# Loading taps and first expert weights in halves of 64 partitions between pairs of x loads

## The chip, the cores and the metric

The kernel runs on one core of a Trainium2 chip. The metric is the time of one execution on the device in microseconds; the time before is the median of three runs. The profile is of one execution, and its times count from the start of its span.

## The reference

A per-head softmax over seven taps weights a causal window of seven tokens; the result goes through a soft mixture of eight experts with four slots each.

```
# x: (8, 3584, 192), weight_gen: (8, 3584, 8 heads, 7 taps)
w = exp(weight_gen - max over taps);  w = w / (sum over taps + 1e-9)
out[b,s,h,:] = sum over k of w[b,s,h,k] * x_padded[b, s+k, h,:]     # six zeros ahead of x
x2 = out.reshape(28672, 192)
logits = x2 @ phi                                   # 32 slots
d = exp(logits - max over tokens); d = d / (sum over tokens + 1e-9)
slot_input = d.T @ x2                               # (8 experts, 4 slots, 192)
slot_out[e] = relu(slot_input[e] @ w1[e]) @ w2[e]   # F = 1024
c = softmax over slots of logits
return c @ slot_out
```

## The kernel before

The work has three stages. The first runs the convolution, the logits and a running softmax over tokens (an online maximum with rescaling, so that `d.T @ x2` is summed as the tokens pass). The second runs the experts on 32 slots. The third multiplies the per-token slot weights with the experts' outputs and stores the result.

**Tiling of the first stage.** A batch's 3584 tokens are cut into tiles of 26; each needs 32 rows of x. Sixteen tiles make an x tile in SBUF, loaded in four DMAs of 32 partitions each (`loadx`, L156): DMA h fills partitions 32h to 32h+31 with the heads h of both halves of the model dimension, so that x stands as a block diagonal whose other blocks were zeroed once. There are 69 x tiles in a ring of five slots (`NXS`). Four tiles make a group, two groups a pair; TensorE works in 35 blocks of four pairs, so a block uses two x tiles. The weights of the convolution come in 35 chunks, one for each block. A chunk's taps are one load over 128 partitions (`loadw`, L160) into one of three buffers. Then follow a chain over three engines: VectorE's maximum (`top`, L171), GpSimd's subtraction (L175), ScalarE's exponential (L179), GpSimd's sum in three steps (L188 to L190), VectorE's reciprocal (L194), GpSimd's product into `wide` (L202), and VectorE's transposition into one of three `band` buffers (L206). TensorE's convolution of a block (`cv`, L230) reads the chunk's band and two x tiles. In each second block TensorE also computes the logits of a unit of eight pairs (`ls`, L281); VectorE takes their maximum (`mx`, L288; `mq`, L290), TensorE spreads it over the partitions (`acb`, L306), VectorE reduces it (`nm`, L310), ScalarE takes exponentials and TensorE sums the slots' inputs (`acb`, L346). The transpositions `pt` (L250) stand between.

**What sets the order.** All loads are issued by SyncE (SP), one after the other, in the order in which the program lists them. For block k the list has: the taps of chunk k+4 (for k = 0, of chunks 3 and 4), the x tiles 2k+5 and 2k+6 (for k = 0 tiles 4 and 5, then `phi`, then tile 6), and now and then a piece of the first expert weights (w1a for the first 128 rows of w1, w1b for the other 64), of which 24 pieces of 128 partitions are spread over the x tiles, two for five tiles. An x tile waits until its slot's old tile was convolved, a chunk's taps until the buffer's old chunk was exponentiated. TensorE's order is the list's too. The orders on VectorE, ScalarE and GpSimd are made by a planner in the kernel (`model`): it goes through the listed operations with a cost and a delay for each, takes at each step the most urgent one that is ready by its own account, and the engines then run that order as it stands. A change to loads in the list therefore changes the order on these engines too.

`op` states for each operation what it reads and writes by names, such as `("w", buffer, half of the chunk)` for taps and `x_of(t)` for an x tile.

Of the kernel before, what the change touches and what calls it, by code (L numbers as in the profile page):

```python
# [30 lines left out]
NS, E, SE, F = 32, 8, 4, 1024  # L31
# [14 lines left out]
def place(t):  # L46
    return t % NXS if t else NXS - 1
# [3 lines left out]
def conv_soft_moe(ctx, tc, xh, wh, phi, w1a, w1b, w2, out):  # L51
    nc = tc.nc
    V, A, G, P, SY = nc.vector, nc.scalar, nc.gpsimd, nc.tensor, nc.sync
# [57 lines left out]
    NTM, NCV, NPT, NTAP, NEX, NBAND = 2, 3, 3, 3, 2, 3  # L111
# [3 lines left out]
    taps = [fix.tile([128, CH, T, KT], F32, name=f"taps{i}") for i in range(NTAP)]  # L115
# [34 lines left out]
    qneg = keep.tile([128, 4], F32, name="qneg")  # L150
    q0 = keep.tile([128, 1], F32, name="q0")
    mq = keep.tile([128, 5], F32, name="mq")
    def loadx(t):

        for h in range(4):
            SY.dma_start(xbd[32 * h : 32 * h + 32, place(t), h], xh[t, h])  # L156

    def loadw(c):
        n = min(CH, NG // 4 - CH * c)
        SY.dma_start(taps[c % NTAP][:, 0:n], wh[c, :, 0:n])  # L160

    ALL = slice(0, CH)
    tops, tsums = {}, {}

    def each(t, n):
        return t.unsqueeze(3).to_broadcast([128, n, T, KT])

    def tap_top(c, b=ALL):
        n = b.stop - b.start
        m = tops[c, b.start] = pa.tile([128, CH, T], F32, tag="top", name=f"top{c}_{b.start}")[:, 0:n]  # L170
        V.tensor_reduce(out=m, in_=taps[c % NTAP][:, b], axis=AX.X, op=ALU.max)  # L171

    def tap_sub(c, b=ALL, eng=G):
        t = taps[c % NTAP][:, b]
        eng.tensor_tensor(out=t, in0=t, in1=each(tops.pop((c, b.start)), b.stop - b.start),  # L175
                          op=ALU.subtract)

    def tap_exp(c, b=ALL):
        A.activation(exps[c % NEX][:, b, :, 0:KT], taps[c % NTAP][:, b], AF.Exp)  # L179
# [11 lines left out]

    def tap_inv(c, b=ALL):
        m = tsums[c, b.start]
        V.reciprocal(m, m)  # L194

    def tap_mul(c, b=ALL, eng=G):

        n = b.stop - b.start
        m = tsums[c, b.start][:, 0:n] if (c, b.start) in tsums else tsums[c, 0][:, b]
        w = wide[:, b]  # L200
        dst = bass.AP(w.tensor, w.offset, [w.ap[0], [T * 32, n], [33, T], [1, KT]])
        eng.tensor_tensor(out=dst, in0=exps[c % NEX][:, b, :, 0:KT], in1=each(m, n), op=ALU.mult)  # L202
# [212 lines left out]
        SY.dma_start(w2_at(e, 0, FC), w2[:, e])  # L415

    def pace(e, what, src):
        op(PO, 0.15, [what], [("w2", e), x_of(NSG - NXS + e // 2)], mark, e, src)
        op(SP, 0.4, [("w2", e)], [], loadw2, e)

    logit, dispatched = {}, {}
    for u in range(1, final + 1):
        k, n = UNITS[u][0] // Q, -(-UNITS[u][1] // Q)
# [27 lines left out]

    VE, AC, PO, TE, SP = "VE", "AC", "PO", "TE", "SP"
    op(SP, 0.65, [], [("w", 0, 0), ("w", 0, 1)], loadw, 0, late=2.6)
    op(SP, 0.65, [], [("w", 1, 0), ("w", 1, 1)], loadw, 1, late=2.6)
    op(SP, 2.6, [], [x_of(0)], loadx, 0, late=2.8)
    op(SP, 0.6, [], [("w", 2, 0), ("w", 2, 1)], loadw, 2, late=3.0)
    op(SP, 1.9, [], [x_of(1)], loadx, 1, late=3.0)
    for t, es in ((2, (PO, AC, AC, AC)), (3, (PO, AC, VE, AC)), (NXS, (PO, PO, AC, AC))):
        for h, e in enumerate(es):
            op(e, 0.77, [], [("z", t, h)], clear, place(t), h, {PO: G, AC: A, VE: V}[e])  # L460
        if t < NXS:
            op(SP, 1.9, [("z", t, h) for h in range(4)], [x_of(t)], loadx, t, late=3.0)
# [82 lines left out]
    for k in range(BLOCKS):  # L545
        ps = range(Q * k, min(Q * (k + 1), PAIRS))
        for p in ps:
            if p == ps[0] + 3 and k in dispatched:
                weigh(dispatched[k])
            if p == ps[min(2, len(ps) - 1)] and k in logit:  # L550
                scores(logit[k])
            op(TE, 0.75 if p == ps[0] else 0.72, conv_reads(p), [("cv", p % NCV)], conv, p)
            op(AC, 0.48, [], [("cv", p % NCV), tm_of(p)], conv_out, p)
        for c in range(3, NCH):
            if k == max(0, c - 2):
                chain(c)
        for c in range(NTAP, NCH):
            if k == max(0, c - 4):
                op(SP, 0.4, [], [("w", c % NTAP, b) for b in range(CH)], loadw, c, late=4.0)
        for t in range(NSG):  # L560
            if (SGG * t + SGG - 1) // (2 * Q) == k:
                if t + NXS < NSG:
                    for i in (NXS - 1, NXS) if t == 0 else (t + NXS,):
                        op(SP, 2.0, [("z", i, h) for h in range(4)], [x_of(i)], loadx, i, late=3.0)
                    if t == 0:
                        op(SP, 0.45, [], ["phi"], SY.dma_start, phi_sb, phi, late=3.0)
                for j in range(2 * (E + E // 2)):
                    if 2 + 5 * j // 2 == t:
# [21 lines left out]
    v, n = final - 1, UNITS[final][1]  # L590
# [86 lines left out]
    for e, cost, late, preds, *_ in ops:  # L677
        t = max([free.get(e, 4.0)] + [goal[j] + ops[j][1] + ops[j][2] + HOP for j in preds])
# [43 lines left out]
    h = EARLY  # L722
# [109 lines left out]
    late = sorted((4 * i + k, h, k) for i, h in enumerate(range(EARLY + 3, len(STEPS))) for k in range(7))  # L832
# [99 lines left out]
```

## Time and profile before

| | us |
|---|---|
| median of three runs | 310.02 |
| lowest and highest run | 309.0, 312.22 |
| the profiled execution's own time | 308.94 |
| its span in the profile | 307.2 |
| first stage, until the last convolution | 222 |
| experts | from about 222 to 250 |
| output | from about 250 to the end |

The profiled execution takes 1.74 us more than its span. Of the data, 46.21 MB are read and 22.04 MB written. A waiting time in the profile's list of waits is idle time of the engine just ahead of the instruction that is named first, and what is named second ended it.

### The profile page before, as it was taken

How to read it: one execution, taken by the hardware profiler on the slowest of the kernel's cores; microseconds unless marked ns; L12 is line 12 of the kernel's file. 1: busy time of each engine (PE TensorE's matmuls, PEld its weight loads, DVE VectorE, ACT ScalarE, POOL GpSimd, SP SyncE). 2: the span in 40 equal slices, each digit the busy share in tenths (PEclk: the TensorE clock that was granted, in tenths of full speed). 3: DMA queues.
4: the chain of work that ended last, by engine and by line, in shares of the span. 5: the costliest groups of instructions: out<-in, count | busy, mean ns of one | idle time of the engine just before them, and what ended most of it. 6: DMA issues, size and time to landing. Idle time of an engine off the chain costs nothing.

```text
span 307.2 us, 15262 instructions
## 1 busy us (share of the span) xinstructions
PE 265.4 (86%) x6646; PEld 213.6 (70%) x6646; DVE 197.8 (64%) x337; ACT 190.3 (62%) x399; POOL 146.5 (48%) x254
## 2 busy tenths in 40 slices
PE   8898996999998999899899989999999888899100
PEld 8887975889887988789788878898768622233000
DVE  8867738775975957868478568573158489994100
ACT  9886673767685778667566666675422188786300
POOL 8856456654568194774654553520027345540000
PEclk9999998999999999999999999999999999879555
DMA  6758666867675767767567667657647079999994
GB/s 184 217 171 236 201 199 195 208 178 207 197 211 150 225 188 207 207 192 212 168 183 212 189 185 211 189 156 227 217 121 296 2 303 403 399 398 398 399 399 177
DMA packets 30161, 69.24 MB, mean 225 GB/s; under 512 B 6288, under 2 KB 11152, under 8 KB 30096
## 3 DMA queue, kind: packets, MB, share of 16 engines
q1 hardware_dynamic: 30096, 68.28, 69.2%
q8 instruction: 52, 0.85, 1.1%
q14 instruction: 13, 0.11, 0.1%
HBM read 46.21 MB, written 22.04 MB: 222 GB/s over the span
## 4 chain that ended last, share of the span: by engine, by line
PE 73%; DVE 6%; DMA 6%; issue 5%; ACT 2%; POOL 2%; DVEq 0%; POOLq 0%; ACTq 0%
PE cv L230 31%; PE pt L250 15%; PE ls L281 8%; PE acb L346 8%; PE po L818 5%; DMA out<-big 4%; PE so L763 2%; PE hpb L742 2%; PE acb L306 2%; DMA taps<-wh 2%; DVE big L825 1%; ACT big L825 1%; DVE band L206 1%; DVE big L362 1%; DVE cT L404 1%
## 5 line engine op out<-in xcount | busy, mean ns | idle before, releaser
L230 PE MATMUL cv<-big,band 128*26 128x96 f32 x4416 | 112.0, 250 | 4.0 <-issue 2.6
L230 PEld LDWEIGHTS cv<-big,band 128*26 128x26 f32 x4416 | 100.8, 130 | 13.8 <-issue 8.1
L236 ACT COPY tm<-cv 128x384 f32<-128x384 f32 x138 | 66.5, 484 | 62.8 <-PE cv L230 62.5
L206 DVE STREAM_TRANSPOSE band<-wide 128x1664 f32<-128x1664 f32 (+1 forms) x37 | 65.4, 1771 | 6.1 <-POOL wide L202 6.0
L250 PE MATMUL pt<-ident,tm 122*128 122x122 f32 x414 | 51.0, 273 | 0.0
L257 ACT COPY cm<-pt 128x416 f32<-128x416 f32 x103 | 48.1, 512 | 1.7 <-PE pt L250 0.6
L250 PEld LDWEIGHTS pt<-ident,tm 122*128 122x128 f32 x414 | 44.7, 145 | 2.3
L202 POOL TENSOR_TENSOR wide<-exps,sum 128x364 f32<-128x364 f32 (+1 forms) x36 | 28.4, 791 | 24.9 <-DVE sum L194 18.6
L818 PE MATMUL po<-cT,so 32*128 32x442 f32 (+3 forms) x256 | 35.4, 644 | 5.6 <-DVE big L825 3.0
L175 POOL TENSOR_TENSOR taps<-taps,top 128x364 f32<-128x364 f32 (+1 forms) x36 | 28.5, 793 | 18.3 <-DVE top L171 17.9
L825 ACT COPY big<-po 128x884 f32<-128x884 f32 (+2 forms) x33 | 28.5, 894 | 9.3 <-PE po L818 5.3
L188 POOL TENSOR_TENSOR si<-exps 128x208 f32<-128x208 f32 x32 | 20.2, 632 | 28.4 <-ACT exps L179 28.0
L818 PEld LDWEIGHTS po<-cT,so 32*128 32x128 f32 (+1 forms) x256 | 12.3, 172 | 27.5 <-ACT big L825 15.7
L281 PE MATMUL ls<-cm,phi_sb 128*32 128x208 f32 x544 | 29.1, 338 | 2.0 <-issue 1.9
L346 PE MATMUL acb<-tm,dt 128*32 128x193 f32 x544 | 27.4, 328 | 3.3 <-issue 3.3
L288 DVE TENSOR_REDUCE mx<-ls 128x1 f32<-128x416 f32 x17 | 10.0, 588 | 28.1 <-PE ls L281 28.1
L87 POOL TENSOR_TENSOR LT<-LT,rm 128x544 f32<-128x544 f32 (+1 forms) x16 | 17.9, 1119 | 17.0 <-DVE rm L85 17.0
L171 DVE TENSOR_REDUCE top<-taps 128x52 f32<-128x364 f32 (+1 forms) x37 | 17.7, 484 | 12.8 <-DMA taps<-wh 12.0
L281 PEld LDWEIGHTS ls<-cm,phi_sb 128*32 128x32 f32 x544 | 17.8, 109 | 7.9 <-issue 3.6
L346 PEld LDWEIGHTS acb<-tm,dt 128*32 128x32 f32 x544 | 17.8, 110 | 7.4 <-issue 4.7
L99 POOL TENSOR_TENSOR LT<-LT,sm 128x544 f32<-128x544 f32 (+1 forms) x16 | 17.9, 1120 | 6.3 <-DVE sm L97 6.2
L825 DVE COPY big<-po 128x884 f32<-128x884 f32 (+2 forms) x16 | 16.7, 1047 | 6.2 <-ACT big L825 2.2
(113 smaller groups left out, 262.3 us busy)
## 6 DMA issues: line engine op xcount, KB each, us to landing
big<-xh SPq DMA_DIRECT2D x276, 96.0 KB, 3.2
out<-big SPq DMA_DIRECT2D x36, 442.0 KB, 6.9
taps<-wh SPq DMA_DIRECT2D x34, 182.0 KB, 3.7
big<-w SPq DMA_DIRECT2D x8, 768.0 KB, 4.5
out<-big SPq DMA_DIRECT2D x11, 468.0 KB, 4.7
w1a_sb<-w1a SPq DMA_DIRECT2D x16, 256.0 KB, 4.2
w1b_sb<-w1b SPq DMA_DIRECT2D x8, 256.0 KB, 3.6
out<-big SPq DMA_DIRECT2D x2, 234.0 KB, 2.3
```

The costliest lines, as they stand in the source:

```text
L175: eng.tensor_tensor(out=t, in0=t, in1=each(tops.pop((c, b.start)), b.stop - b.start), op=ALU.subtract)
L188: eng.tensor_tensor(out=s, in0=t[:, :, :, 0:4], in1=t[:, :, :, 4:8], op=ALU.add)
L202: eng.tensor_tensor(out=dst, in0=exps[c % NEX][:, b, :, 0:KT], in1=each(m, n), op=ALU.mult)
L206: V.transpose(bands[c % NBAND][:, b].rearrange("p b j l -> p (b j l)"), wide[:, b].rearrange("p b j -> p (b j)"))
L230: P.matmul(cv[32 * blk : 32 * blk + T, o : o + 4 * GW], bands[g // 8 % NBAND][:, g // 4 % CH, :, i], xbd[:, place(t), :, b * GW : (b + 1) ...
L236: copy(tms[u % NTM][:, pr, 1 : 2 * D + 1], cvs[p % NCV][:, 0 : 2 * D])
L250: P.transpose(pt[:, at, 0:TR], tms[u % NTM][0:TR, pr, 1 + 128 * i : 129 + 128 * i], ident[0:TR, 0:TR])
L257: copy(cms[u].rearrange("p a i b j -> p (a i b) j")[:, at : at + n], pts.pop((k, j)).rearrange("p i (b j) -> p (i b) j", j=32)[:, 0:n, 0:T])
L281: P.matmul(lp[32 * blk : 32 * blk + 32, lo:hi, par, 0:T], phi_sb[:, 2 * par + i, :], cm[:, lo:hi, 1 if i else 2 * par, blk, :], start=(i = ...
L346: P.matmul(ac[32 * q : 32 * q + 32], dt[:, g, :], tm[:, g // 2, o : o + D + 1], start=(g < 4), stop=(g + 4 >= 2 * n))
L818: P.matmul(po[dst : dst + hi - lo, at, 0 : n * T], so[32 * q : 32 * q + 32, lo:hi], cT[32 * q : 32 * q + 32, g0 : g0 + n, 0:T], start=True ...
L825: (V.tensor_copy if done[1] % 3 == 1 else A.copy)(ot.rearrange("p (q c) -> p q c", c=n * T), po[:, 0 : len(qs), 0 : n * T])
```

## The change

`loadx` takes a range of DMAs to issue, `loadw` a range of partitions. For k above 0 each x tile is now issued as two pairs of DMAs (partitions 0 to 63, then 64 to 127), and one half of a chunk's taps stands between the pairs: partitions 0 to 63 in the first x tile of a block, 64 to 127 in the second. What is left of the list goes behind the x tiles: for k = 0 this is the second half of chunk 3 and both halves of chunk 4. The first expert weights come in 48 pieces of 64 partitions in place of 24 of 128, four for five x tiles. The first three chunks are loaded as before. An x tile has two names, one for each pair of DMAs; the convolution reads both.

```diff
-    def loadw(c):
+    def loadw(c, r=slice(0, 128)):
         n = min(CH, NG // 4 - CH * c)
-        SY.dma_start(taps[c % NTAP][:, 0:n], wh[c, :, 0:n])
+        SY.dma_start(taps[c % NTAP][r, 0:n], wh[c, r, 0:n])
+
+    def loadw1(j):
+        e, f, r = j // 4, slice(F // 2 * (j // 2 % 2), F // 2 * (j // 2 % 2 + 1)), HALF[j % 2]
+        to, w, e = (w1a_sb, w1a, e) if e < E else (w1b_sb, w1b, e - E)
+        SY.dma_start(to[r, e, f], w[r, e, f])
+    HALF = slice(0, 64), slice(64, 128)
...
-        for c in range(NTAP, NCH):
-            if k == max(0, c - 4):
-                op(SP, 0.4, [], [("w", c % NTAP, b) for b in range(CH)], loadw, c, late=4.0)
-        for t in range(NSG):
-            if (SGG * t + SGG - 1) // (2 * Q) == k:
-                if t + NXS < NSG:
-                    for i in (NXS - 1, NXS) if t == 0 else (t + NXS,):
-                        op(SP, 2.0, [("z", i, h) for h in range(4)], [x_of(i)], loadx, i, late=3.0)
-                    if t == 0:
-                        op(SP, 0.45, [], ["phi"], SY.dma_start, phi_sb, phi, late=3.0)
-                for j in range(2 * (E + E // 2)):
-                    if 2 + 5 * j // 2 == t:
...
+        cs = [c for c in range(NTAP, NCH) if k == max(0, c - 4)]
+        parts = [(c, i) for c in cs for i in range(2)]
+        for t in (2 * k, 2 * k + 1):
+            for i in (NXS - 1, NXS) if t == 0 else (t + NXS,) if t + NXS < NSG else ():
+                for j in range(2):
+                    op(SP, 1.0, [("z", i, h) for h in (2 * j, 2 * j + 1)], [x_of(i)[j]],
+                       loadx, i, (2 * j, 2 * j + 1), late=3.0)
+                    if j == 0 and parts and t:
+                        c, h = parts.pop(0)
+                        op(SP, 0.4, [], [("w", c % NTAP, h)], loadw, c, HALF[h], late=4.0)
+            if t == 0:
+                op(SP, 0.45, [], ["phi"], SY.dma_start, phi_sb, phi, late=3.0)
+            if 2 <= t < NSG:
+                for j in range(48):
+                    if 2 + 5 * j // 4 == t:
+                        op(SP, 0.42, [], [], loadw1, j)
+        for c, h in parts:
+            op(SP, 0.4, [], [("w", c % NTAP, h)], loadw, c, HALF[h], late=4.0)
```

**SP at the start.** The three tap buffers are taps_84 (chunks 0, 3, 6 and so on), taps_85 (chunks 1, 4) and taps_86 (chunks 2, 5). Before, behind the taps of chunk 2:

```order
L156 DMA big<-xh 32x768 x12
L160 DMA taps_84<-wh 128x364
L160 DMA taps_85<-wh 128x364
L156 DMA big<-xh 32x768 x8
L686 DMA phi_sb<-phi 128x128
L156 DMA big<-xh 32x768 x4
L160 DMA taps_86<-wh 128x364
```

Now, behind the taps of chunk 2 (the rows up to chunk 5's second half):

```order
L156 DMA big<-xh 32x768 x20
L695 DMA phi_sb<-phi 128x128
L156 DMA big<-xh 32x768 x2
L160 DMA taps_84<-wh 64x364
L156 DMA big<-xh 32x768 x2
L160 DMA taps_84<-wh 64x364
L160 DMA taps_85<-wh 64x364 x2
L156 DMA big<-xh 32x768 x2
L160 DMA taps_86<-wh 64x364
L156 DMA big<-xh 32x768 x2
L165 DMA w1a_sb<-w1a 64x512
L156 DMA big<-xh 32x768 x2
```

Chunks 3 and 4 stood ahead of x tiles 4, 5, `phi` and x tile 6 and now stand in and behind tile 6; the next row after these is chunk 5's second half, which stood behind tile 6 as a whole and now stands in tile 8.

**VectorE at the start.** The rows from the reciprocal of chunk 2 to the band of chunk 3 (band_90), before:

```order
L194 RECIPROCAL sum_0_325<-sum_0_325 128x52
L171 TENSOR_REDUCE top_0_387<-taps_84 128x52
L171 TENSOR_REDUCE top_0_390<-taps_85 128x52
L206 STREAM_TRANSPOSE band_92<-wide 128x1664
L194 RECIPROCAL sum_0_453<-sum_0_453 128x52
L288 TENSOR_REDUCE mx_525<-ls 128x1
L290 TENSOR_SCALAR mq<-ls,mx_525 128x4
L206 STREAM_TRANSPOSE band_90<-wide 128x1664
```

Now:

```order
L212 STREAM_TRANSPOSE band_92<-wide 128x1664
L294 TENSOR_REDUCE mx_510<-ls 128x1
L296 TENSOR_SCALAR mq<-ls,mx_510 128x4
L177 TENSOR_REDUCE top_0_534<-taps_84 128x52
L316 TENSOR_REDUCE nm_544<-acb 128x1
L177 TENSOR_REDUCE top_0_553<-taps_85 128x52
L333 STREAM_TRANSPOSE dt_564<-dd 128x512
L300 STREAM_TRANSPOSE LT<-ls 128x512
L200 RECIPROCAL sum_0_570<-sum_0_570 128x52
L177 TENSOR_REDUCE top_0_589<-taps_86 128x52
L200 RECIPROCAL sum_0_580<-sum_0_580 128x52
L212 STREAM_TRANSPOSE band_90<-wide 128x1664
```

The maxima of chunks 3 and 4 moved behind the first unit's `mx`, and the band of chunk 3 now stands behind the maximum of chunk 5 (taps_86).

**VectorE at the third unit's maximum.** The rows around the maxima of chunks 8 (taps_86) and 9 (taps_84) and the band of chunk 7 (band_91), before:

```order
L171 TENSOR_REDUCE top_0_928<-taps_86 128x52
L85 TENSOR_REDUCE rm_947<-LT 128x18
L354 SCALAR_TENSOR_TENSOR accS<-accS,al_949,acb 128x193
L194 RECIPROCAL sum_0_951<-sum_0_951 128x52
L171 TENSOR_REDUCE top_0_998<-taps_84 128x52
L206 STREAM_TRANSPOSE band_91<-wide 128x1664
L288 TENSOR_REDUCE mx_1064<-ls 128x1
L290 TENSOR_SCALAR mq<-ls,mx_1064 128x4
```

Now:

```order
L177 TENSOR_REDUCE top_0_963<-taps_86 128x52
L360 SCALAR_TENSOR_TENSOR accS<-accS,al_956,acb 128x193
L200 RECIPROCAL sum_0_958<-sum_0_958 128x52
L212 STREAM_TRANSPOSE band_91<-wide 128x1664
L294 TENSOR_REDUCE mx_1072<-ls 128x1
L296 TENSOR_SCALAR mq<-ls,mx_1072 128x4
L93 TENSOR_REDUCE sm_1093<-LT 128x18
L316 TENSOR_REDUCE nm_1105<-acb 128x1
L200 RECIPROCAL sum_0_1050<-sum_0_1050 128x52
L177 TENSOR_REDUCE top_0_1120<-taps_84 128x52
```

The maximum of chunk 9 moved from ahead of `mx` to behind it.

More of the change, by code (lines that the diff above doesn't have):

```diff
@@ L152, in conv_soft_moe, with loadx @@
     mq = keep.tile([128, 5], F32, name="mq")
-    def loadx(t):
-        for h in range(4):
+    def loadx(t, hs=range(4)):
+        for h in hs:
             SY.dma_start(xbd[32 * h : 32 * h + 32, place(t), h], xh[t, h])
-    def loadw(c):
+    def loadw(c, r=slice(0, 128)):
         n = min(CH, NG // 4 - CH * c)
-        SY.dma_start(taps[c % NTAP][:, 0:n], wh[c, :, 0:n])
+        SY.dma_start(taps[c % NTAP][r, 0:n], wh[c, r, 0:n])
[3 more added lines that the diff above has]
+        SY.dma_start(to[r, e, f], w[r, e, f])
     ALL = slice(0, CH)
+    HALF = slice(0, 64), slice(64, 128)
     tops, tsums = {}, {}
@@ L417, in pace @@
     def pace(e, what, src):
-        op(PO, 0.15, [what], [("w2", e), x_of(NSG - NXS + e // 2)], mark, e, src)
+        op(PO, 0.15, [what], [("w2", e), *x_of(NSG - NXS + e // 2)], mark, e, src)
         op(SP, 0.4, [("w2", e)], [], loadw2, e)
@@ L442, in x_of @@
     def x_of(t):
-        return ("x", place(t))
+        return [("x", place(t), i) for i in range(2)]
     def conv_reads(p):
-        return {x_of(g // SGG) for g in (2 * p, 2 * p + 1)} | {("band", p // 4 % NBAND, p // 2 % CH)}
+        return {x for g in (2 * p, 2 * p + 1) for x in x_of(g // SGG)} | {("band", p // 4 % NBAND, p // 2 % CH)}
     def tm_of(p):
@@ L454, in conv_soft_moe @@
     op(SP, 0.65, [], [("w", 1, 0), ("w", 1, 1)], loadw, 1, late=2.6)
-    op(SP, 2.6, [], [x_of(0)], loadx, 0, late=2.8)
+    op(SP, 2.6, [], x_of(0), loadx, 0, late=2.8)
     op(SP, 0.6, [], [("w", 2, 0), ("w", 2, 1)], loadw, 2, late=3.0)
-    op(SP, 1.9, [], [x_of(1)], loadx, 1, late=3.0)
+    op(SP, 1.9, [], x_of(1), loadx, 1, late=3.0)
     for t, es in ((2, (PO, AC, AC, AC)), (3, (PO, AC, VE, AC)), (NXS, (PO, PO, AC, AC))):
@@ L461, in conv_soft_moe @@
         if t < NXS:
-            op(SP, 1.9, [("z", t, h) for h in range(4)], [x_of(t)], loadx, t, late=3.0)
+            op(SP, 1.9, [("z", t, h) for h in range(4)], x_of(t), loadx, t, late=3.0)
     for i in range(NCV):
@@ L556, in conv_soft_moe @@
                 chain(c)
-        for c in range(NTAP, NCH):
-            if k == max(0, c - 4):
-                op(SP, 0.4, [], [("w", c % NTAP, b) for b in range(CH)], loadw, c, late=4.0)
-        for t in range(NSG):
-            if (SGG * t + SGG - 1) // (2 * Q) == k:
-                if t + NXS < NSG:
-                    for i in (NXS - 1, NXS) if t == 0 else (t + NXS,):
-                        op(SP, 2.0, [("z", i, h) for h in range(4)], [x_of(i)], loadx, i, late=3.0)
-                    if t == 0:
-                        op(SP, 0.45, [], ["phi"], SY.dma_start, phi_sb, phi, late=3.0)
-                for j in range(2 * (E + E // 2)):
-                    if 2 + 5 * j // 2 == t:
-                        e, f = j // 2, slice(F // 2 * (j % 2), F // 2 * (j % 2 + 1))
-                        to, w, e = (w1a_sb, w1a, e) if e < E else (w1b_sb, w1b, e - E)
-                        op(SP, 0.4, [], [], SY.dma_start, to[:, e, f], w[:, e, f])
+        cs = [c for c in range(NTAP, NCH) if k == max(0, c - 4)]
[16 more added lines that the diff above has]
+            op(SP, 0.4, [], [("w", c % NTAP, h)], loadw, c, HALF[h], late=4.0)
         for p in ps:
```

## The prediction

> **What bounds the kernel now.** I read the page first, then the busy time of each engine by stretches, then the chain of waits, and last the timelines of SP, VectorE and TensorE around the places where the chain leaves TensorE. The page's busy shares and its chain, by engine:
>
> ```profile
> PE 265.4 (86%) x6646; PEld 213.6 (70%) x6646; DVE 197.8 (64%) x337; ACT 190.3 (62%) x399; POOL 146.5 (48%) x254
> PE 73%; DVE 6%; DMA 6%; issue 5%; ACT 2%; POOL 2%; DVEq 0%; POOLq 0%; ACTq 0%
> ```
>
> The stretches of the first stage and of the output (length, busy time of PE, PEld, DVE, ACT, POOL, granted clock, DMA share, GB/s):
>
> ```profile
> 13.00:50.00 37.00, 32.47 (x992) 28.46 (x992) 24.57 (x36) 26.09 (x61) 20.81 (x38) 1.00 0.68 198
> 50.00:100.00 50.00, 48.05 (x1347) 42.41 (x1351) 36.12 (x60) 32.72 (x75) 32.26 (x54) 0.97 0.68 195
> 100.00:150.00 50.00, 47.60 (x1417) 41.87 (x1412) 35.70 (x60) 34.34 (x79) 28.28 (x49) 1.00 0.70 203
> 150.00:205.00 55.00, 53.35 (x1585) 47.56 (x1577) 38.70 (x61) 37.09 (x83) 26.30 (x49) 1.00 0.65 187
> 250.00:307.20 57.20, 30.77 (x228) 10.68 (x224) 30.13 (x44) 29.76 (x42) 14.17 (x13) 0.73 0.95 369
> ```
>
> TensorE bounds the first stage: it is idle 4.5 us between 13 and 50, and 1.95 + 2.4 + 1.65 = 6.0 us between 50 and 205. The last row is the output, where the DMAs are busy 95% of the time; the change leaves the experts and the output alone. So a gain can come only from some 10.5 us of idle TensorE in the first stage, and a loss from new idle time there.
>
> **Term 1, the start.** SP's timeline, before:
>
> ```profile
> 9.58 1.25 SPq L160 DMA_DIRECT2D taps<-wh  x2
> 10.93 4.37 SPq L156 DMA_DIRECT2D big<-xh  x8
> 15.35 1.44 SPq L686 DMA_DIRECT2D phi_sb<-phi  x1
> 16.88 1.78 SPq L156 DMA_DIRECT2D big<-xh  x4
> ...
> 110.71 1.77 SPq L156 DMA_DIRECT2D big<-xh  x4
> 112.53 0.42 SPq L686 DMA_DIRECT2D w1a_sb<-w1a  x1
> ```
>
> The last two rows price an issue: four undisturbed ones of 32 partitions take 112.53 - 110.71 = 1.82 us, 0.455 each with the step to the next, and one of 128 partitions takes 0.42 without that step. What one of 64 costs no row shows; it lies between these two, which hardly differ. The page's times from issue to landing, with count and size:
>
> ```profile
> big<-xh SPq DMA_DIRECT2D x276, 96.0 KB, 3.2
> taps<-wh SPq DMA_DIRECT2D x34, 182.0 KB, 3.7
> w1a_sb<-w1a SPq DMA_DIRECT2D x16, 256.0 KB, 4.2
> ```
>
> So a half costs SP a whole issue: 0.455 us. A half of the taps is 91 KB, near an x load, whose landing takes 3.2 us; the whole takes 3.7. I take 3.7, since the halves go out in a dense row. The Trainium skill, page "DMA: Bandwidth & Descriptors", section "Rules for kernel authors", says of two transfers to disjoint partition halves "Don't bother — they serialize", and speaks against this change. By that rule a pair lands no sooner than the whole, and the sum is the one below; by the row of the x loads the start would be 0.5 us shorter.
>
> Chunks 3 and 4 were issued at 9.58, ahead of x tile 4. Now tiles 4 and 5 and `phi` go first. They don't get earlier for it: tile 4 waits for the convolution of its slot's old tile, so I keep 16.88 for tile 6. From there the order has x, x, chunk 3's first half, x, x, its second half: the sixth issue, at 16.88 + 5 x 0.455 = 19.2. Chunk 5's second half is the seventeenth: 24.2 if nothing is disturbed, and with one or two long issues (as `phi`'s 1.44 us against 0.42) some 25.1 to 26. It lands 3.7 us later, at 28.8 to 29.7. VectorE and TensorE before:
>
> ```profile
> 14.73 0.91 DVE L171 TENSOR_REDUCE top<-taps 128x52 f32<-128x364 f32 x2
> ...
> 21.55 1.90 DVE L206 STREAM_TRANSPOSE band<-wide 128x1664 f32<-128x1664 f32 x1
> ...
> 24.00 2.21 PE L230 MATMUL cv<-big,band 128*26 128x96 f32 x96
> ```
>
> Chunk 3's band was done at 23.45 and its block's convolution began at 24.00, without a wait. In VectorE's new order that band stands behind chunk 5's maximum. So: landing 28.8 to 29.7, maximum 0.5, reciprocal 0.5, band 1.9 gives 31.7 to 32.6; the convolution begins 7.7 to 8.6 us late. I take 8.2. The bounds come from a late chunk's chain, the quickest part of the trace, from maximum to start of the band:
>
> ```profile
> 170.71 0.53 DVE L171 TENSOR_REDUCE top<-taps 128x52 f32<-128x364 f32 x1 [2.45 <-DMA taps<-wh]
> 178.56 1.87 DVE L206 STREAM_TRANSPOSE band<-wide 128x1664 f32<-128x1664 f32 x1
> ```
>
> That is 9.7 us to the band's end. Chunk 3 alone, landing at 22.9, would be done at 32.6, or about 2 us sooner where the other engines stand idle and serve it at once: 6.5 us late at the least. With another long issue or a landing of 5 us it is 10. Everything behind the convolution on TensorE moves with it, x loads included, which wait for slots; nothing hides it.
>
> **Term 2, the clock.** The trace shows what an idle TensorE costs besides. At 47 us VectorE waited for chunk 9's taps, ahead of the unit's maximum:
>
> ```profile
> 35.11 1.45 PE L250 MATMUL pt<-ident,tm 122*128 122x122 f32 x12
> 36.49 2.21 PE L230 MATMUL cv<-big,band 128*26 128x96 f32 x96
> ...
> 47.08 0.53 DVE L171 TENSOR_REDUCE top<-taps 128x52 f32<-128x364 f32 x1 [3.67 <-DMA taps<-wh]
> 47.53 1.90 DVE L206 STREAM_TRANSPOSE band<-wide 128x1664 f32<-128x1664 f32 x1
> 49.36 0.55 DVE L288 TENSOR_REDUCE mx<-ls 128x1 f32<-128x416 f32 x1
> ...
> 50.31 0.36 PE L306 MATMUL acb<-mq,sel 128*128 128x5 f32 x2 [2.77 <-DVE mq L290]
> 50.53 1.96 PE L250 MATMUL pt<-ident,tm 122*128 122x122 f32 x12
> 52.42 3.27 PE L230 MATMUL cv<-big,band 128*26 128x96 f32 x96
> ...
> 52.40:54.00 1.60, 1.60 (x41) 1.58 (x44) 1.60 (x2) 0.01 (x1) 0.71 (x1) 0.50 0.83 241
> ```
>
> After 2.77 us of idleness the granted clock was 0.50 for a while; the same work took 1.96 and 3.27 in place of 1.45 and 2.21, 1.6 us more. A new stall of 8 us is cold at its end too: I take 1.5 us; 0.8 to 3.1 if it lasts half or twice as long.
>
> **Term 3, the old stall goes.** Its 2.77 and 1.6, together 4.3 us, came from chunk 9's maximum standing ahead of `mx` on VectorE. In the new order it stands behind. Chunk 8's still stands ahead, but TensorE is then some 8 us later, and its taps go out with x tiles that follow TensorE. I take -4.3; 0 if a new wait takes its place.
>
> **Term 4, the rest of the stage.** The change adds 32 tap issues (two halves for 32 of 35 chunks) and 24 issues of expert weights: 56 x 0.455 = 25.5 us of SP. Before, SP issues 276 x loads, 35 of taps, 24 of expert weights and `phi` until about 206 us, 153 us at 0.455, and waits, above all:
>
> ```profile
> SPq L156 <- PE cv L230: 13.5, 26, 1.7
> SPq L156 <- PE pt L250: 7.6, 12, 1.4
> SPq L160 <- ACT tm L236: 5.0, 9, 1.3
> SPq L160 <- ACT exps L179: 4.4, 4, 1.4
> SPq L156 <- PE acb L306: 4.3, 7, 1.7
> ```
>
> These 34.8 us cover the 25.5: a fuller SP finds its slots already free. That is the cover, and it leaves some 9 us; what is neither issue nor wait in the 206 us, some 18 us, holds smaller waits and long issues like `phi`'s. Added waits are few: an x pair or a half that waits for its slot holds up only what is behind it on SP, which is the next half and the x loads. What can be late next is the taps: a chunk's second half is issued one x tile and more later against TensorE, about 6 us (a block's time). Chunk 20 shows the margin:
>
> ```profile
> 109.25 1.36 SPq L160 DMA_DIRECT2D taps<-wh  x1
> 113.19 0.53 DVE L171 TENSOR_REDUCE top<-taps 128x52 f32<-128x364 f32 x1
> 126.84 1.87 DVE L206 STREAM_TRANSPOSE band<-wide 128x1664 f32<-128x1664 f32 x1
> 133.32 1.55 PE L230 MATMUL cv<-big,band 128*26 128x96 f32 x64
> ```
>
> The band was done at 128.7, 4.6 us ahead of its use, and the chain took 15.5 us where 9.7 are enough: 10.4 us of room for 6 us of delay. Long issues of 1 to 1.5 us take part of the other 4. I take 1.5 us for the places where they don't fit; the bounds are 0 (all fits) and 8 (a third of SP's added 25.5 us is not covered). Two names for an x tile and two semaphores for a chunk add a wait instruction here and there on engines with idle time: 0.
>
> **Sum.** 8.2 + 1.5 - 4.3 + 1.5 = +6.9 us on the profiled execution's 308.94 us (span 307.2 and 1.74 around it): 315.8, say 316 us. The median of the runs before is 1.1 us above the profiled one, so against it the loss is 5.8 us, 1.9%.
>
> **Rivals.**
> - *SP becomes the bound.* For: 153 + 25.5 + 18 us nearly fill the 206, and an in-order queue can't use all its waits. Against: the 34.8 us of waits. At 8 in place of 1.5: 322 us.
> - *The stall at the start is short.* The bound of 6.5 holds, the clock recovers at once, the old stall goes and the rest fits: 308.94 + 6.5 - 4.3 = 311 us, no difference. For: in the stall all other engines are free. Against: the row of chunk 5 on VectorE.
> - *Faster.* One mechanism: maxima no longer stand ahead of TensorE's work on VectorE, and the idle 6.0 us between 50 and 205 go with the old 4.3. With the start at 6.5 that is 308.94 + 6.5 - 10.3 = 305 us. It decides only if the start costs less than 7 us with the clock and nearly all idle time goes.
> - *The halves load the DMA engines.* Taps and expert weights are a third of the stage's bytes; at twice their time the DMA share of 0.68 would be 0.9, landings go from 3.7 towards 5 us, term 1 grows by 1.3 and term 4 by 2: 319 us. Against: the x loads, all of this kind, land in 3.2 us. The Trainium skill, page "SBUF — State Buffer", section "Door 1: The DMA port swizzle", says that 64 partitions reach only half of the ports; no run here shows it yet.
> - *Nothing happens.* No: the order at the start has moved, and no wait stands ahead of chunk 3's old place that would hold it back there.
>
> **Chances.** The forecast 0.5 (its own range 313 to 319), SP as the bound 0.18, loaded DMAs 0.08, short stall 0.19, faster 0.05. The time is that of the forecast, 316. The range of 310 to 323 takes in the short stall and SP's bound and leaves out about 2 in 10. A measurement of this kernel tells about 1% from no change, here 306.9 to 313.1 us. Faster 0.05; the same 0.21 (the short stall, and a little of the forecast's lower end); slower 0.74.
>
> **What would show it.** Right: TensorE idle for about 8 us ahead of the convolution at 24 us, with VectorE at chunk 5's maximum behind a DMA; a granted clock of 0.5 just behind; no wait of `mq` near 60 us; SP's issue time 25 us more and its waits on TensorE and ScalarE shrunk by about as much. Wrong: chunk 3's band ahead of 29 us, tap loads that land in 5 us, waits of the convolution on bands or x loads all through the stage, or issues of 64 partitions that take other than about 0.42 us.

## The result: 13% slower, and the profile after

The changed kernel takes 351.71 us (median of 4 runs, 349.4 to 353.65), the kernel before, run beside it, 311.12 us (309.0 to 316.0): the ratio is 1.133 (95% interval 1.121 to 1.144), 41 us more. The ratio leaves out one run of before (316.0 us) that fell in a slower state of the chip. The forecast was 316 us, some 6 us above the runs of before: the sign was right, and the size was far off.

The page's busy shares and the first line of its chain, after:

```profile
PE 277.4 (79%) x6646; PEld 224.6 (64%) x6646; DVE 198.3 (57%) x337; ACT 190.0 (54%) x399; POOL 146.5 (42%) x254
PE 47%; DMA 14%; DVE 14%; SPq 8%; POOL 5%; issue 4%; ACT 2%; DVEq 0%; ACTq 0%; POOLq 0%
```

TensorE was 73% of the chain and is 47%; DMA, VectorE, GpSimd (POOL) and SP's queue, which had 14% together, now hold 41%. The same stretches as before (length, busy time of PE, PEld, DVE, ACT, POOL, granted clock, DMA share, GB/s), with the end of the first stage, now at 265 us:

```profile
13.00:50.00 37.00, 28.21 (x828) 25.38 (x829) 20.75 (x29) 21.75 (x52) 15.94 (x30) 0.91 0.55 156
50.00:100.00 50.00, 43.31 (x1205) 38.09 (x1203) 27.54 (x46) 28.61 (x65) 22.78 (x38) 0.93 0.56 157
100.00:150.00 50.00, 38.58 (x1041) 34.13 (x1041) 30.39 (x48) 26.20 (x60) 25.82 (x44) 0.91 0.59 168
150.00:205.00 55.00, 49.21 (x1383) 43.66 (x1383) 31.34 (x51) 32.83 (x75) 25.43 (x44) 0.93 0.56 158
205.00:264.00 59.00, 49.45 (x1280) 43.79 (x1284) 30.07 (x48) 30.23 (x69) 18.95 (x40) 0.88 0.61 174
292.00:350.20 58.20, 32.13 (x232) 11.28 (x225) 30.93 (x45) 30.42 (x43) 14.19 (x13) 0.70 0.94 368
```

The loss is spread over the whole first stage: TensorE is idle 5.8 to 11.4 us in every such stretch, and in each the granted clock is 0.88 to 0.93 where it was 0.97 to 1.00. The output is about as long as it was (58.2 us against 57.2). The DMA engines are less busy than before (0.55 to 0.61 against 0.65 to 0.70), so they are not what holds the stage up. What VectorE and TensorE wait for, after (time in total, how often, the longest):

```profile
DVE top L177 <- DMA taps<-wh: 68.2, 27, 6.4
PE acb L312 <- DVE mq L296: 26.7, 10, 5.0
PE cv L236 <- DVE band L212: 9.2, 2, 8.2
```

VectorE waited 12.0 us for taps before, and waits 68.2 now. The convolution waits for a band at the start and hardly again. The place where TensorE stands is `acb<-mq`, the unit's maximum, and the timeline of the three engines at one such place shows how the delay gets there:

```profile
64.42 0.47 SPq L160 DMA_DIRECT2D taps<-wh  x1
...
68.27 0.53 DVE L177 TENSOR_REDUCE top<-taps 128x52 f32<-128x364 f32 x1 [4.57 <-DMA taps<-wh]
...
72.40 0.55 DVE L294 TENSOR_REDUCE mx<-ls 128x1 f32<-128x416 f32 x1
...
73.36 0.56 PE L312 MATMUL acb<-mq,sel 128*128 128x5 f32 x2 [3.98 <-DVE mq L296]
73.78 2.68 PE L256 MATMUL pt<-ident,tm 122*128 122x122 f32 x12
```

SP issues a second half late; VectorE, in its fixed order, stands 4.57 us at the chunk's maximum; `mx` stands behind that, and TensorE stands 3.98 us for `mq`. Then the granted clock is 0.50 (73.3 to 77 us) and the transposes take 2.68 in place of 1.45 us. Why SP is late is what the runs were made for.

### The profile page after: what moved, and what is told of

It reads as the page before. It is cut to its first block, busy times and chain, and to the rows that moved or that the text cites. A ratio compares the mean times of both kernels' runs of the same rounds, so it can differ in the third digit from the quotient of the medians.

```text
span 350.2 us, 15360 instructions
## 1 busy us (share of the span) xinstructions
PE 277.4 (79%) x6646; PEld 224.6 (64%) x6646; DVE 198.3 (57%) x337; ACT 190.0 (54%) x399; POOL 146.5 (42%) x254
## 4 chain that ended last, share of the span: by engine, by line
PE 47%; DMA 14%; DVE 14%; SPq 8%; POOL 5%; issue 4%; ACT 2%; DVEq 0%; ACTq 0%; POOLq 0%
PE cv L236 19%; PE pt L256 10%; DMA taps<-wh 8%; SPq L156 6%; DVE band L212 5%; PE acb L352 5%; PE ls L287 4%; DMA out<-big 3%; PE po L827 3%; DMA big<-xh 3%; POOL taps L181 2%; POOL wide L208 2%; PE so L772 2%; PE hpb L751 2%; PE acb L312 2%
## 5 line engine op out<-in xcount | busy, mean ns | idle before, releaser
L236 PE MATMUL cv<-big,band 128*26 128x96 f32 x4416 | 118.1, 262 | 10.4 <-DVE band L212 9.2
L236 PEld LDWEIGHTS cv<-big,band 128*26 128x26 f32 x4416 | 108.2, 134 | 20.3 <-DVE band L212 9.9
L242 ACT COPY tm<-cv 128x384 f32<-128x384 f32 x138 | 65.6, 482 | 56.5 <-PE cv L236 56.3
L177 DVE TENSOR_REDUCE top<-taps 128x52 f32<-128x364 f32 (+1 forms) x37 | 18.4, 501 | 73.6 <-DMA taps<-wh 68.2
L256 PE MATMUL pt<-ident,tm 122*128 122x122 f32 x414 | 56.8, 292 | 2.5 <-ACT tm L242 2.5
L256 PEld LDWEIGHTS pt<-ident,tm 122*128 122x128 f32 x414 | 49.5, 156 | 5.2 <-ACT tm L242 3.0
L208 POOL TENSOR_TENSOR wide<-exps,sum 128x364 f32<-128x364 f32 (+1 forms) x36 | 28.4, 790 | 14.9 <-DVE sum L200 12.9
L185 ACT ACTIVATE exps<-taps 128x364 f32<-128x364 f32 (+1 forms) x37 | 18.4, 497 | 28.0 <-POOL taps L181 25.7
L312 PE MATMUL acb<-mq,sel 128*128 128x5 f32 (+1 forms) x34 | 6.8, 271 | 30.3 <-DVE mq L296 26.7
L312 PEld LDWEIGHTS acb<-mq,sel 128*128 128x128 f32 x34 | 5.7, 209 | 32.9 <-issue 13.8
L352 PE MATMUL acb<-tm,dt 128*32 128x193 f32 x544 | 25.9, 327 | 0.4 <-DVE dt L333 0.4
L324 ACT ACTIVATE dd<-ls,nm 128x416 f32<-128x416 f32 x17 | 10.4, 612 | 25.0 <-DVE nm L316 24.7
L99 POOL TENSOR_TENSOR LT<-LT,sm 128x544 f32<-128x544 f32 (+1 forms) x16 | 17.9, 1120 | 11.8 <-DVE sm L97 11.7
```

Source lines behind the costliest of these rows:

```text
L236: P.matmul(cv[32 * blk : 32 * blk + T, o : o + 4 * GW], bands[g // 8 % NBAND][:, g // 4 % CH, :, i], xbd[:, place(t), :, b * GW : (b + 1) ...
L242: copy(tms[u % NTM][:, pr, 1 : 2 * D + 1], cvs[p % NCV][:, 0 : 2 * D])
L256: P.transpose(pt[:, at, 0:TR], tms[u % NTM][0:TR, pr, 1 + 128 * i : 129 + 128 * i], ident[0:TR, 0:TR])
L352: P.matmul(ac[32 * q : 32 * q + 32], dt[:, g, :], tm[:, g // 2, o : o + D + 1], start=(g < 4), stop=(g + 4 >= 2 * n))
```

## The experiments

Two theories stood at first. **S**: SP's issuing sets the pace of the first stage. **P**: the new places do it (each chunk complete one x tile later, and VectorE's order that goes with it). Where no number of runs is given, a time below is that of one execution. These scatter (the kernel before: 305.86 to 316.0 us over all its runs), so a difference of 5 us between two of them decides nothing.

**Whole pieces at the places of the second halves.** From the changed kernel: `parts = list(cs)`, 128 partitions at once, 24 weights in place of 48.

```diff
-                    if j == 0 and parts and t:
-                        c, h = parts.pop(0)
-                        op(SP, 0.4, [], [("w", c % NTAP, h)], loadw, c, HALF[h], late=4.0)
+                    if j == 0 and parts and (t if k == 0 else t % 2):
+                        c = parts.pop(0)
+                        op(SP, 0.4, [], [("w", c % NTAP, b) for b in range(CH)], loadw, c, late=4.0)
```

> Taps whole (128 partitions) where the changed kernel has their second half, between the pairs of an x tile; expert weights in 24 whole pieces. The later places stay, the 56 added issues and all loads of 64 partitions go. Theory S (SP is the bound, because a load of 64 partitions costs it 0.52 us and makes the next x load 0.16 us longer, 0.68 in all against 0.47 for a whole one): SP has 56 x 0.68 + 56 x 0.21 = 50 us less to issue, so TensorE bounds again and only the later start stays: 314 to 319 us. Theory P (the later places of the taps and the order that the planner makes of them cost the time): 340 us or more.

It took 309.35 us (before, beside it, 311.03). P asked for 340 us or more: it falls. What the later places cost is timed below.

**As many pieces, cut along the row, each of 128 partitions.**

```diff
-        SY.dma_start(taps[c % NTAP][r, 0:n], wh[c, r, 0:n])
+        SY.dma_start(taps[c % NTAP][:, b], wh[c, :, b])
...
-        e, f, r = j // 4, slice(F // 2 * (j // 2 % 2), F // 2 * (j // 2 % 2 + 1)), HALF[j % 2]
+        e, f, r = j // 4, slice(F // 4 * (j % 4), F // 4 * (j % 4 + 1)), slice(0, 128)
```

> The changed kernel with its places and its number of loads, but a chunk's taps are cut between its two halves along the row (128 partitions x 728 bytes) and the expert weights into 128 partitions x 1024 bytes. S with the price tied to 64 partitions: each piece costs 0.47 and the next x nothing more, 112 x 0.21 = 24 us less than the changed kernel: about 328 us (322 to 334). S with the price tied to the number of issues alone: 350 us. P: 350 us.

330.0 us: 20.6 above the whole pieces, and 21.7 below the changed kernel. So the loss has two parts of about equal size: one for the number of pieces, one for their 64 partitions.

**Only the taps in halves, and only the weights in halves.** In each, the other kind is loaded whole at its old places: the weights in 24 pieces, the taps ahead of the block's x tiles (so in the second of the two kernels the start is as before, too).

```diff
-                for j in range(48):
-                    if 2 + 5 * j // 4 == t:
+                for j in range(24):
+                    if 2 + 5 * j // 2 == t:
```

```diff
-        parts = [(c, i) for c in cs for i in range(2)]
+        parts = []
+        for c in cs:
+            op(SP, 0.4, [], [("w", c % NTAP, b) for b in range(CH)], loadw, c, late=4.0)
```

> Only the taps in halves of 64 partitions at the changed kernel's places; expert weights in 24 whole pieces. S: 48 x 0.68 - 24 x 0.47 = 21 us less of SP than in the changed kernel: about 330 us. P: 345 to 352 us, since the taps' places are those of the changed kernel.

> Only the expert weights in 48 halves; taps whole and ahead of the block's x tiles, as before. S: 64 x 0.68 - 32 x 0.47 = 28 us less of SP than in the changed kernel, and the start as before: 315 to 323 us. P: 309 to 312 us, since the taps are where they were.

333.27 and 321.19 us: 23.9 and 11.8 above the whole pieces. Together that is 35.7, and both at once cost 42.4. That fits an SP whose free time is used up once and not twice, but 6.7 us between sums of single executions prove little.

**The start undone.** Chunks 3 and 4 whole and ahead of x tile 4, the rest as changed.

```diff
-        parts = [(c, i) for c in cs for i in range(2)]
+        parts = [(c, i) for c in cs if k for i in range(2)]
+        for c in cs if k == 0 else ():
+            op(SP, 0.4, [], [("w", c % NTAP, b) for b in range(CH)], loadw, c, late=4.0)
```

> The changed kernel with taps chunks 3 and 4 whole and ahead of x tile 4, as before the change; every later place and every half as in the changed kernel. If each late piece costs by itself, the start's stall (8.23 us ahead of the conv of block 3) goes and the time falls by it: about 342. If the issues on SP's queue bound the rest of the first stage, SP has the same work less two issues, and only what the start's stall cost that SP could not use otherwise comes back: 345 to 350, with the waits for `mq` larger than in the changed kernel.

352.22 us. TensorE's timeline at the start, of this kernel:

```profile
23.74 2.21 PE L236 MATMUL cv<-big,band 128*26 128x96 f32 x96
```

The stall of 8 us and the cold clock behind it are gone, and the time is the same: in this kernel the stall costs nothing that shows.

**The weights issued by ScalarE.** The same halves, by another engine's queue.

```diff
-        SY.dma_start(to[r, e, f], w[r, e, f])
+        A.dma_start(to[r, e, f], w[r, e, f])
...
-                        op(SP, 0.42, [], [], loadw1, j)
+                        op(AC, 0.5, [tm_of(ps[0])], [], loadw1, j, due=4.0)
```

> The changed kernel with the 48 half loads of the first expert weights issued by ScalarE; SP keeps the x loads and the half taps. Bytes, pieces and partitions of all transfers are the same. If SP's issuing is the bound, SP has 48 issues fewer and is left with what the kernel with halved taps alone less 24 whole weights has: 318 to 330. If the transfers themselves bound the stage (64 partitions, more descriptors), it stays at 345 to 355. If ScalarE's time counts (48 issues of about 0.5 us), its part comes on top and the waits for ScalarE's copies grow: 335 to 345.

326.13 us: 25.6 us come back though the same bytes move in the same pieces. This is the plainest evidence for S. What ScalarE pays for it shows in TensorE's waits of this kernel, 8.1 us for its copies, against 2.5 in the changed one:

```profile
PE pt L256 <- ACT tm L242: 8.1, 7, 2.0
```

**The planner told SP's true prices.** A pair of x loads 1.25 in place of 1.0, a half 0.55 in place of 0.40 or 0.42; SP's order is the same.

```diff
-                    op(SP, 1.0, [("z", i, h) for h in (2 * j, 2 * j + 1)], [x_of(i)[j]],
+                    op(SP, 1.25, [("z", i, h) for h in (2 * j, 2 * j + 1)], [x_of(i)[j]],
...
-                        op(SP, 0.42, [], [], loadw1, j)
+                        op(SP, 0.55, [], [], loadw1, j)
```

> The changed kernel with the planner told what SP's loads cost in its trace: a pair of x loads 1.25 instead of 1.0, a half of taps or weights 0.55 instead of 0.40 to 0.42. SP's order stays; the other engines' order is planned for later pieces. If SP's issuing alone sets the pace: 347 to 353. If VectorE's order, planned for taps that come earlier than they do, makes the lateness larger on its way to TensorE: 335 to 345, with the waits of TensorE for `mq` (26.7 us in the changed kernel) down to half.

345.1 us, 2% less and at the edge of the second range; one execution doesn't tell whether the order is worth that. TensorE's waits in this kernel:

```profile
PE cv L236 <- DMA big<-xh: 18.5, 13, 2.8
PE cv L236 <- DVE band L212: 16.7, 18, 6.2
PE acb L312 <- DVE mq L296: 4.1, 8, 1.0
```

The waits for `mq` went from 26.7 to 4.1 us, and waits of the convolution for bands and x came in their place. The order decides where TensorE stands; the time hardly follows it.

**Halves side by side.** The kernel before, with each whole piece from chunk 3 on replaced by two halves back to back, and 0.8 in place of 0.4 as the planner's price of a chunk's taps.

```diff
-        SY.dma_start(taps[c % NTAP][:, 0:n], wh[c, :, 0:n])
+        for r in (slice(0, 64), slice(64, 128)) if c >= NTAP else (slice(0, 128),):
+            SY.dma_start(taps[c % NTAP][r, 0:n], wh[c, r, 0:n])
...
-                op(SP, 0.4, [], [("w", c % NTAP, b) for b in range(CH)], loadw, c, late=4.0)
+                op(SP, 0.8, [], [("w", c % NTAP, b) for b in range(CH)], loadw, c, late=4.0)
...
-                        op(SP, 0.4, [], [], SY.dma_start, to[:, e, f], w[:, e, f])
+                        for r in (slice(0, 64), slice(64, 128)):
+                            op(SP, 0.4, [], [], SY.dma_start, to[r, e, f], w[r, e, f])
```

> The kernel before with the taps from chunk 3 on and the first expert weights in halves of 64 partitions, the two halves back to back in the places of the whole ones. As many added issues as in the changed kernel, but a load of x follows a pair of halves and not each half. If the price is the issue's own and the next load's (0.52 and 0.16), the added time is 20.6 for the issues, as in the kernel of 128-partition pieces, and about half of the 21.7 for the shape: 335 to 345. If it is alternating with x that costs, 315 to 330. If halves are dear wherever they are, 350.

345.84 us, 1 us above the first range: alternating with x is not the price, and the halves are dear side by side too. SP's timeline of this kernel:

```profile
104.39 1.11 SPq L688 DMA_DIRECT2D w1a_sb<-w1a  x2
```

Two halves take 1.11 us, where two undisturbed x loads take 0.89 (below).

**Cut at partition 96 in place of 64.** As many pieces, at the same places, with the same bytes.

```diff
-    HALF = slice(0, 64), slice(64, 128)
+    HALF = slice(0, 96), slice(96, 128)
```

> The changed kernel with its halves cut at partition 96 instead of 64: pieces of 96 and of 32 partitions, same count, same places, same bytes. If the dear issue belongs to 64 partitions alone, the pieces cost what 128 and 32 partitions cost (0.465 a step) and the time is that of the pieces along the row, 328 to 334. If any piece that is cut by partitions is dear, 348 to 355. If only the pieces of 96 are dear, between: 338 to 345.

331.22 us: the whole price of the shape is gone, and the time is that of the pieces cut along the row. So, of the widths tried here (32, 64, 96 and 128), it belongs to 64 partitions, and not to cutting by partitions. SP's timelines show the price itself. The changed kernel:

```profile
118.82 0.47 SPq L165 DMA_DIRECT2D w1a_sb<-w1a  x1
119.39 0.99 SPq L156 DMA_DIRECT2D big<-xh  x2
120.48 0.47 SPq L160 DMA_DIRECT2D taps<-wh  x1
121.00 1.04 SPq L156 DMA_DIRECT2D big<-xh  x2
122.09 0.47 SPq L165 DMA_DIRECT2D w1a_sb<-w1a  x1
```

The kernel cut at 96:

```profile
108.46 0.42 SPq L165 DMA_DIRECT2D w1a_sb<-w1a  x1
108.98 0.83 SPq L156 DMA_DIRECT2D big<-xh  x2
109.91 0.36 SPq L160 DMA_DIRECT2D taps<-wh  x1
110.32 0.89 SPq L156 DMA_DIRECT2D big<-xh  x2
111.25 0.42 SPq L165 DMA_DIRECT2D w1a_sb<-w1a  x1
```

Six issues without a wait take 3.27 us (118.82 to 122.09) with halves of 64 and 2.79 us (0.465 each) without. That is 0.24 us more for each half here, most of it on the load that follows: a pair of x loads lasts 1.04 behind a half of the taps and 0.89 behind a piece of 96. The medians from 13 to 206 us give 0.21: a half of the taps steps 0.52 us to the next issue against 0.46, and the x load behind it 0.63 against 0.47. Over 112 halves this is 24 to 27 us; 20 us of it arrived in the time.

**Bare loads: how much SP has free.** In the kernel of whole pieces, each place of a first half gets a load of 32 partitions by 4 bytes that nothing reads: 24 at the weights' places (the lines below), or 56 at the weights' and the taps' places.

```diff
+    def more():
+        j = next(extra) % 28
+        SY.dma_start(dum[:, j : j + 1], wh[0, 0:32, 0, 0, 0:1])
...
-                        op(SP, 0.4, [], [], loadw1, j)
+                        op(SP, 0.42, [], [], *((loadw1, j) if j % 2 else (more,)))
```

> Whole pieces of taps and first expert weights where the changed kernel has second halves, timed: the zero point of the line. One look gave 309.35. 307 to 312, within 1% of before, is expected by both theories.

> The whole pieces at the same places, and where the changed kernel has the first halves of the weights, 24 loads of 32 partitions by 4 bytes into a tile that nothing reads: 11.2 us of SP's issuing at 0.465 and hardly a byte. If SP's waits cover added issuing first (as the prediction had it, up to 25.5 us), the time stays within 1% of the whole pieces. If every issue counts from the first, 11 us more: 319 to 322. If the waits cover a part (the kernel with halved weights alone kept 11.8 of 21 us), 4 to 7 more.

> The same with 56 bare loads, one in the place of each first half of taps and weights: 26 us of SP's issuing. If the number of issues on SP's queue is what made the pieces cut along the row slow (330.0), this comes to the same, 326 to 333. If it was the pieces themselves (two landings to wait for, more packets), 310 to 316.

| kernel, median of 13, 10, 4 and 4 runs | us | ratio to before (95% interval) |
|---|---|---|
| before | 309.22 | |
| whole pieces | 312.27 | 1.010 (1.005 to 1.015) |
| and 24 bare loads | 315.97 | 1.018 (1.008 to 1.028) |
| and 56 bare loads | 331.9 | 1.067 (1.060 to 1.073) |

The ratios are not the quotients of these medians, which take in every run. 56 loads of hardly a byte cost 19.6 us, as much as the 56 added pieces of the kernel cut along the row (20.6). So the loss needs neither bytes nor a second landing to wait for: added issues alone make it. And the line bends: the first 24 (11.2 us at 0.465) cost 3.7 us, the next 32 (14.9 us) cost 15.9. By the ratios it is 2.4 and 15; the first of these is hardly clear of nothing, since the intervals overlap. As the first 24 stand at the weights' places and the next 32 at the taps', the runs don't separate the number from the place. What SP issued between 13 and 206 us shows how full it is. Issues by kind, with count, size and median time to landing, of the kernel with 56 bare loads:

```profile
big<-xh SPq DMA_DIRECT2D x225, 96.0 KB, 3.3
taps<-wh SPq DMA_DIRECT2D x29, 182.0 KB, 3.8
w1a_sb<-w1a SPq DMA_DIRECT2D x16, 256.0 KB, 3.6
w1b_sb<-w1b SPq DMA_DIRECT2D x6, 256.0 KB, 4.1
dum<-wh SPq DMA_DIRECT2D x51, 0.1 KB, 3.3
phi_sb<-phi SPq DMA_DIRECT2D x1, 64.0 KB, 3.5
```

These are 328 issues in 193 us, 0.588 us each. In the same stretch the kernel cut along the row issues 327 and the one cut at 96 issues 328, whatever they carry. Kernels with equally many issues and nearly the same time must show nearly the same count; that it is a ceiling rests on SP's own time, of which it waits 17 to 22 us in these three and issues for the rest. The whole pieces issue 304 and the kernel before 310, so by this estimate SP has room for some 20 more. The changed kernel, in the same stretch:

```profile
big<-xh SPq DMA_DIRECT2D x205, 96.0 KB, 2.8
taps<-wh SPq DMA_DIRECT2D x53, 91.0 KB, 2.5
w1a_sb<-w1a SPq DMA_DIRECT2D x32, 128.0 KB, 3.2
w1b_sb<-w1b SPq DMA_DIRECT2D x8, 128.0 KB, 3.4
phi_sb<-phi SPq DMA_DIRECT2D x1, 64.0 KB, 3.1
```

299 issues, 0.645 each: 50 fewer x loads than before (255), and x tiles are what the stage consumes. An estimate from these counts: it wants 304 + 56 = 360 in this stretch, is 61 short, and 61 x 0.645 = 39 us; against the whole pieces it is 39.4 us slower. This is bookkeeping and no proof: fewer issues in a fixed stretch and a longer time are two sides of one thing.

**Whole pieces, with chunks 3 and 4 early.** The start of the kernel before, the later places of the change; then the same with the weights in 12 pieces. Against the first experiment:

```diff
-        parts = list(cs)
+        parts = list(cs) if k else []
+        for c in cs if k == 0 else ():
+            op(SP, 0.4, [], [("w", c % NTAP, b) for b in range(CH)], loadw, c, late=4.0)
```

```diff
-        e, f, r = j // 2, slice(F // 2 * (j % 2), F // 2 * (j % 2 + 1)), slice(0, 128)
+        e, f, r = j, slice(0, F), slice(0, 128)
```

> Whole pieces at the places of the changed kernel's second halves, but chunks 3 and 4 ahead of x tile 4. The run of whole pieces at the same places gave 309.35 with a stall of 6.79 us at the start. If that stall costs the time fully, 302 to 304; if the later stage takes it up (the issues set the pace), 307 to 310.

> The kernel of whole pieces with chunks 3 and 4 early, timed in rounds against the kernel before. One look gave 304.37 beside 308.53. If the places are worth what they seem, 303 to 305 and 1 to 2.5% less than before; if that look was luck, within 1% of before.

> The same kernel with the first expert weights in 12 pieces of twice the size instead of 24: 12 issues fewer, 5.6 us of SP's issuing. If SP's issuing still bounds the first stage with whole pieces, the time falls by up to 5 to 299 to 301. If TensorE's own work bounds it by now (it was busy 97% of the stage), 303 to 306. If the larger pieces delay the taps and x behind them, 306 to 310.

The first execution took 304.37 us beside 308.53; timed over 10 runs, it is 309.41 beside 309.85, a ratio of 0.996 (0.990 to 1.002): no difference from before. The 304.37 was luck. Against the whole pieces with the late start (1.010, 1.005 to 1.015), the two intervals don't overlap: the late start costs some 4 us there, and the later places of the other chunks cost nothing that shows. TensorE's stall in the kernel with the late start:

```profile
30.18 4.07 PE L236 MATMUL cv<-big,band 128*26 128x96 f32 x96 [5.73 <-DVE band L212]
```

With 12 pieces it is 313.17 us, 1.012 (1.007 to 1.017). Twelve issues fewer don't help, so with whole pieces SP does not seem to be the bound. It is no clean test: the larger pieces land in 5.0 us where the smaller take 3.9, and why they harm was not studied. No kernel of these beats the one before.

## Why the prediction was wrong, point by point

**What bounded the kernel before**: right, TensorE. It didn't stay so: by the estimate above SP was some 20 issues short of its ceiling, and the change added 56.

**Terms 1 and 2, start and clock**: right as events, though the number of term 1 is in part luck. SP, VectorE and TensorE, after:

```profile
15.08 1.59 SPq L156 DMA_DIRECT2D big<-xh  x2
...
26.68 0.47 SPq L160 DMA_DIRECT2D taps<-wh  x1
...
29.15 0.53 DVE L177 TENSOR_REDUCE top<-taps 128x52 f32<-128x364 f32 x1 [2.89 <-DMA taps<-wh]
29.98 1.85 DVE L212 STREAM_TRANSPOSE band<-wide 128x1664 f32<-128x1664 f32 x1
31.89 2.46 PE L236 MATMUL cv<-big,band 128*26 128x96 f32 x56 [8.23 <-DVE band L212]
```

The band stood behind chunk 5's maximum and the convolution began at 31.89, within 31.7 to 32.6; the stall is 8.23 us (8.2 predicted). But on the way errors cancelled: tile 6 went out at 15.08 (16.88 forecast), the sixteen issues from there to chunk 5's second half took 11.6 us (8.2 to 9.1 forecast, long issues included), and that half landed within 2.5 us of its issue (3.7 forecast). As terms of the sum they were void: with the start undone the time stayed at 352.22, since a stage that is bound by SP gets TensorE's stall for nothing. With whole pieces, where the time is near that of before, the late start does cost, some 4 us. So the price of a stall holds only while TensorE is the bound. The clock came back as a toll on later stalls: its mean went from 0.945 to 0.886, and the same TensorE instructions were busy 277.4 us in place of 265.4.

**Term 3, the old stall**: TensorE's timeline at the third unit's maximum, after, and its waits for `mq` in all, before:

```profile
57.20 0.36 PE L312 MATMUL acb<-mq,sel 128*128 128x5 f32 x2 [1.49 <-DVE mq L296]
```

```profile
PE acb L306 <- DVE mq L290: 3.2, 2, 2.8
```

That wait is 1.49 us where it was 2.77, and no cold clock follows (1.00 from 57.2 to 59 us). But such waits sum to 26.7 us now, against 3.2: the 4.3 us were not gained.

**Term 4** is the step that failed: "These 34.8 us cover the 25.5: a fuller SP finds its slots already free." The runs put three findings in its place.

First, the waits give way only in part. SP's largest waits of the changed kernel between 13 and 206 us:

```profile
SPq L156 <- PE cv L236: 6.5, 11, 1.8
SPq L156 <- PE pt L256: 5.7, 10, 1.7
SPq L160 <- ACT tm L242: 4.3, 7, 1.5
SPq L160 <- ACT cm L263: 1.6, 4, 0.5
```

All of SP's waits in this stretch sum to 40 us before, 34 with whole pieces, 23 with 24 bare loads, 22 with 56 and 22 in the changed kernel (some 30 when its last x load is issued, at 250 us): they shrink to about 20 us and stop. So at most half of the cover was real, and 24 bare loads use it up. Whole pieces with the early start, as fast as before, wait 28 us, so even the 40 vary. Why the rest stays was not tried. The rows name TensorE and ScalarE as the ones that free the slots; they are late themselves when SP is late, and a wait of that kind grows with SP's delay instead of hiding it. That reading fits, but it is an argument.

Second, the price of an issue. 0.455 was read from undisturbed rows; with the long issues and the waits that stay, SP needs 0.588 for each when it is saturated (so this holds the first finding in it). The long issues were seen and not explained: between 13 and 206 us, 26 to 31 last over 0.7 us without a recorded wait (before, whole pieces, 56 bare loads, changed), 21 to 29 us beyond 0.42 for each. Of these 114, 112 run during a 16 KB transfer on q8, a queue that the profile calls instruction, with which about a fifth of all issues coincide; the other two run during one of 8 KB on q14, the other such queue, and no issue outside both lasts over 0.61 us. No run tried whether these transfers hold SP up. Judged by 0.588, the kernel before was close to its limit: its 310 issues by 206 us take 182 of 193 us. The forecast set 153 us of issuing and 18 us of other time against 206.

Third, the half. The prediction bounded its issue by neighbours of 32 and 128 partitions and noted that these hardly differ; 64 doesn't lie between them. The cost is 0.21 to 0.24 us more for each half, and shows mostly on the load behind it, about 20 us in all. It had named this as something that would prove it wrong ("issues of 64 partitions that take other than about 0.42 us").

The rest of term 4, that the later places fit into the room that the taps have, held: with whole pieces and the early start they cost nothing that shows.

**Rivals.** *SP becomes the bound* was the true one. It was priced at 8 us more than nothing because a third of 25.5 us was thought not to be covered; without the shape's price it is 20 us, and with it 40. *The halves load the DMA engines* is refuted: halves of taps land in 2.5 us where the whole took 3.7, and 56 loads of hardly a byte lose as much as pieces with bytes. The Trainium skill, page "SBUF — State Buffer", section "Door 1: The DMA port swizzle", has 64 partitions reach half of the ports; no slower landing came of it here. The Trainium skill, page "DMA: Bandwidth & Descriptors", section "Rules for kernel authors", says not to bother with halves, "they serialize". The kernel with halves side by side agrees, in its landings between 13 and 206 us:

```profile
taps<-wh SPq DMA_DIRECT2D x52, 91.0 KB, 3.1
```

With 0.52 us between the two issues, a pair is complete some 3.6 us after its first issue, no sooner to speak of than the whole's 3.7. What the halves cost shows in no landing, but in the queue that issues them. The *short stall* and the *faster* case had no part in it.

## What to carry to other kernels

Before adding DMAs to a queue, count what it issues in a saturated stretch, waits and long issues included, and compare it with the count now: SP here had room for some 20 issues in 193 us, by the estimate above, though its waits summed to 40 us. Waits of an in-order queue for slots that its own transfers help to free are no cover until a run has shown it: add bare loads and see where the time bends. Where a load must be split, try other widths than 64 partitions, and price each shape from a row of its own.

## What the runs showed of the hardware that was not expected

- A load of 64 partitions makes SP's issuing dearer, by 0.21 to 0.24 us for the load and the one behind it together, and a cut at 96 and 32 or along the row doesn't. The time follows: 351.7 against 331.2 and 330.0 us. What in the chip makes the difference no run shows.
- A load of 32 partitions by 4 bytes occupies SP as long as one of 128 partitions by 2 KB, 0.42 us. SP's timeline of the kernel with 56 bare loads:

```profile
117.01 0.42 SPq L167 DMA_DIRECT2D dum<-wh  x1
117.53 0.84 SPq L156 DMA_DIRECT2D big<-xh  x2
...
120.92 0.42 SPq L172 DMA_DIRECT2D w1a_sb<-w1a  x1
```

- Those 128 bytes land in 3.3 us, as 96 KB of x do in the same kernel.
- The saturated rate is 0.588 us for each issue, SP's waits of some 20 us included, where an undisturbed one takes 0.465.
- Issues over 0.7 us long without a recorded wait, 26 to 31 in 193 us, coincide with 16 KB transfers on the queue q8: 112 of the 114 in four kernels.
